# Dynamic convolution and two MLPs on one core: block 1's taps summed by TensorE, VectorE alone on the second weights, PSUM banks added one at a time, six blocks ahead, a new table of early tasks

## The chip, the cores and the metric

One core of a Trainium2 chip. The metric is device time in microseconds (us); lower is better. A profiled execution has its own time, and its trace covers a span a little shorter than that. Engines: PE (TensorE; PEld is its weight load), DVE (VectorE), ACT (ScalarE), POOL (GpSimd), and SP, which issues the DMAs. Each takes its instructions in the order in which the program lists them.

## The reference, cut to what matters

```python
# x (2, 4096, 192), weight_gen (2, 4096, 8, 7): float32, S = 4096, D = 192, H = 8, K = 7
w = softmax(weight_gen, axis=-1)                     # over the 7 taps
x_pad = np.concatenate([zeros((B, 6, D)), x], axis=1)
out[b, s, h, :] = sum_k w[b, s, h, k] * x_pad[b, s + k, h, :]     # 24 channels to a head
x = out.reshape(8192, 192)
x = (np.maximum(x @ w_in, 0.0) ** 2) @ w_out         # first MLP, 192 -> 2048 -> 192
h = x @ w_in2
return (h / (1.0 + np.exp(-1.702 * h))) @ w_out2     # second MLP
```

The four weight matrices arrive as float64 words.

## The kernel before, in words

**Tiling.** Token t of the flat 8192 lies on partition t // 64. The 64 tokens of a partition are cut into 16 blocks j of 4 (`TB`), so a block is 512 tokens. All matmul operands are split into a high part (rounded to `fp32r`) and a low part (the remainder); a product is the sum of three (high-high, low-high, high-low) or, in the second matrix, two of five column groups.

**A pair.** The unit of the main loop is (l, j, q): layer l, block j, one eighth q of the 2048 hidden columns. There are 2 x 16 x 8 = 256. For each, `mm_in` (L301) does 18 matmuls into a PSUM tile `h` of two banks; ACT makes `g` from it (L313 and L314: relu and square, or L316: gelu) and the high part `gh` (L320, `high_g`); DVE makes the low part `gl` (L326, `low_g`); and `mm_out` (L331) adds its product to the block's output `p`, two pairs later (`LAG`). For blocks 0 and 1 of layer 0 one `p` tile is used with 10 matmuls of 128 rows; everywhere else two `p` tiles, each from one half of the partitions, with 20 matmuls of 64 rows. `p0` and `p1` have one buffer each, two banks each, and a pool hands a tile on as a whole: the next block's first matmul into `p1` waits until both banks of the old `p1` have been read.

**Pair order.** L428 to L434: blocks 0 and 1 of layer 0 in two halves each (16 pairs), then layer 0 of the blocks below `LEAD`, then layer 1 of block j - `LEAD` alternating with layer 0 of block j, then the last `LEAD` blocks of layer 1. I number pairs from 0 in this order.

**Before a block's first pair.** `load_x` fetches the tokens and the six before them; `mul_task` multiplies by one tap's weights (L223, tile `pr`), `add` (L235) sums the seven products on DVE; `transposed` (L267) turns the sum with 16 small matmuls into a PSUM tile `tx` out of the same two buffers as `h`; `split` (L250) makes `xs`, high by ACT (L257), low by DVE (L258); `swap` (L261) copies halves across partitions by DMA. For block 0 alone (`plan_summed`, L461) the products are not added on DVE: each is transposed into the same PSUM tile, which adds them up. `softmax_tasks` (L173) make the tap weights `wg` for two blocks.

**Weights.** A `Chunk` (L88; 16 for each layer) is loaded, and then decoded from float64: ACT takes the magnitude (L104), DVE shifts and masks (L109, L110, L114: `t_bits`), multiplies and adds (L118, L121: `t_sum`), ACT rounds the high part (L138 or L156), DVE makes the low part (`wil`, L142; `wo`, L160 and L161). The addition of L121 runs on DVE for layer 0 and on POOL for layer 1.

**After a block's last pair.** `sums` (L349): ACT copies `p0` to `t` (L356) while DVE copies `p1` to `s` (L357); one step later DVE adds them (L363). Layer 0 then swaps and adds halves (L374, L378); layer 1 transposes (`u`, L407), and writes out (L412 to L420).

**Order of the work.** Every piece is a task in `todo`, keyed by a step; steps -20 to -1 come before the main loop, which has two steps to a pair: at the even step `low_g` of the pair before, `mm_in`, tasks; at the odd step `mm_out` of the pair two back, tasks, `high_g`. What an engine does, it does in that order. The numbers at L441 to L537 say at which step a task stands. `st` (L63) is one pool of ten buffers for raw weights, decoded weights, products, `s`, `t` and outputs.

Of the kernel before, what the change touches and what calls it, by code (L numbers as in the profile page):

```python
# [17 lines left out]
def kernel(  # L18
# [69 lines left out]
    class Chunk:  # L88
# [27 lines left out]
        def t_sum(self):  # L116
# [4 lines left out]
            (nc.vector if self.l == 0 else nc.gpsimd).tensor_add(self.s, self.s, self.u)  # L121
            del self.raw, self.low, self.high, self.u

        def tasks(self):
            return [self.t_words, self.t_bits, self.t_sum, self.t_high, self.t_low]
# [223 lines left out]
    def sums(l, j, hold):  # L349

        def t_copy():
            s = hold["s"] = work(f"s{l}_{j}", [P, 2, N])
# [1 line left out]
            if len(p) == 2:
                t = hold["t"] = work(f"t{l}_{j}", [P, 2, N])
                nc.scalar.copy(t, p[0])  # L356
                nc.vector.tensor_copy(s, p[1])  # L357
            else:
                nc.scalar.copy(s, p[j])

        def t_add():
            if "t" in hold:
                nc.vector.tensor_add(hold["s"], hold["s"], hold.pop("t"))  # L363

        return [t_copy, t_add]
# [95 lines left out]
    def plan_summed(j, i0, i1):  # L461

        hold = {}
        at(i0 - 6, lambda: hold.update(x=load_x(j)))
        for k in range(KT):
            at(
                i0 + k * (i1 - 2 - i0) // KT,
                mul_task(j, hold, k), lambda k=k: transposed(j, hold, k, k == 0, k == KT - 1),
            )
        at(i1 - 2, lambda: hold.pop("x"), *split_tasks(j, hold))  # L470

    def plan_softmax(s, i):
        at(i - 8, lambda: load_wg(s))
        for n, t in enumerate(softmax_tasks(s)):
            at(i + n, t)

    def plan_weights(chunk, when, lead):

        at(when[0] - lead, chunk.t_load)
        for t, i in zip(chunk.tasks(), when):  # L480
            at(i, t)
# [102 lines left out]
```

## Time and profile before

| | |
|---|---|
| median of 3 runs | 1212.54 us (1211.09 to 1214.18) |
| the profiled execution | 1212.81 us |
| its span in the trace | 1210.8 us |
| mean granted clock of TensorE | 0.981 |
| first matmul of pair 0 / of pair 16 / of pair 48 | 21.58 / 120.52 / 283.12 us |
| last matmul of pair 255 ends | about 1202.5 us |
| a pair where nothing waits | 4.31 us (blocks 0 and 1 of layer 0: 4.78 us) |

Three tables of the profile are read below. A row of the timeline is: start, duration, engine, source line, operation, output<-inputs, shapes, and in brackets how long the engine had been idle and what ended that. A row of the groups is a line's instructions of one kind: how many, busy us in total, mean ns of one, and the idle time of the engine before them. A row of the windows is one stretch of the span with each engine's busy time in it and the mean granted clock, 1.00 being 2.4 GHz and 0.50 being 1.2 GHz.

### The profile page before, as it was taken

How to read it: one execution, taken by the hardware profiler on the slowest of the kernel's cores; microseconds unless marked ns; L12 is line 12 of the kernel's file. 1: busy time of each engine (PE TensorE's matmuls, PEld its weight loads, DVE VectorE, ACT ScalarE, POOL GpSimd, SP SyncE). 2: the span in 40 equal slices, each digit the busy share in tenths (PEclk: the TensorE clock that was granted, in tenths of full speed). 3: DMA queues.
4: the chain of work that ended last, by engine and by line, in shares of the span. 5: the costliest groups of instructions: out<-in, count | busy, mean ns of one | idle time of the engine just before them, and what ended most of it. 6: DMA issues, size and time to landing. Idle time of an engine off the chain costs nothing.

```text
span 1210.8 us, 23439 instructions
## 1 busy us (share of the span) xinstructions
PE 1154.9 (95%) x10176; PEld 1087.1 (90%) x10176; DVE 723.0 (60%) x822; ACT 781.4 (65%) x821; POOL 30.8 (3%) x26
## 2 busy tenths in 40 slices
PE   4698899989999999999999999999999999999997
PEld 3466778879999999999999999998999999999997
DVE  7998897874646646465655646466464643433333
ACT  2676767857757675676757577576756757555553
POOL 1000111310000000000000000000000000000000
PEclk8899999989999999999999999999999999999999
DMA  7421223301121110112120011211101111110010
GB/s 189 113 88 41 88 63 120 87 9 52 31 60 39 41 41 19 52 41 58 32 59 27 23 51 32 60 39 41 41 19 51 34 24 32 28 31 15 18 32 27
DMA packets 29958, 58.90 MB, mean 49 GB/s; under 512 B 4004, under 2 KB 15394, under 8 KB 29856
## 3 DMA queue, kind: packets, MB, share of 16 engines
q1 hardware_dynamic: 29856, 57.41, 17.2%
q8 instruction: 79, 1.29, 0.5%
q14 instruction: 23, 0.19, 0.0%
HBM read 30.13 MB, written 6.29 MB: 30 GB/s over the span
## 4 chain that ended last, share of the span: by engine, by line
PE 83%; DVE 11%; ACT 2%; issue 2%; DMA 2%; SPq 0%; ACTq 0%; DVEq 0%
PE p L344 43%; PE h L307 38%; DVE pr L223 2%; DVE gl L326 2%; DVE pr L235 1%; DVE xs L258 1%; PE tx L278 1%; DMA xt<-in_x_dram 1%; PE u L407 1%; ACT xs L257 1%; ACT gh L320 1%; DMA ro<-in_moe_w_out_dram 1%; DVE uso L110 0%; DVE usi L110 0%; DVE usi L118 0%
## 5 line engine op out<-in xcount | busy, mean ns | idle before, releaser
L326 DVE TENSOR_TENSOR gl<-g,gh 128x1024 fp32r<-128x1024 f32 x256 | 317.3, 1239 | 327.2 <-ACT gh L320 326.9
L344 PE MATMUL p<-gh,wo 64*128 64x512 f32 (+1 forms) x2976 | 468.3, 392 | 11.0 <-DVE s L357 6.0
L307 PE MATMUL h<-xs,wih 64*128 64x512 f32 x3072 | 466.0, 392 | 7.3 <-DVE xs L258 4.1
L344 PEld LDWEIGHTS p<-gh,wo 64*128 64x128 f32 (+1 forms) x2976 | 344.9, 186 | 32.8 <-DVE s L357 7.1
L307 PEld LDWEIGHTS h<-xs,wih 64*128 64x128 f32 x3072 | 342.2, 186 | 30.3 <-PE p L344 7.8
L344 PE MATMUL p<-gl,wo 64*128 64x512 f32 (+1 forms) x1984 | 345.1, 389 | 0.0
L320 ACT CAST gh<-g 128x1024 fp32r<-128x1024 f32 x256 | 268.7, 1050 | 90.5 <-PE p L344 88.1
L344 PEld LDWEIGHTS p<-gl,wo 64*128 64x128 f32 (+1 forms) x1984 | 234.7, 186 | 10.2
L307 PE MATMUL h<-xs,wil 64*128 64x512 f32 x1536 | 231.0, 389 | 1.6 <-DVE wil L142 1.6
L316 ACT ACTIVATE g<-h 128x1024 f32<-128x1024 f32 x128 | 131.7, 1029 | 152.4 <-PE h L307 150.5
L313 ACT ACTIVATE g<-h 128x1024 f32<-128x1024 f32 x128 | 131.6, 1028 | 110.6 <-PE h L307 109.1
L307 PEld LDWEIGHTS h<-xs,wil 64*128 64x128 f32 x1536 | 173.0, 186 | 10.2 <-DVE wil L142 2.0
L314 ACT ACTIVATE g<-g 128x1024 f32<-128x1024 f32 x128 | 135.8, 1061 | 4.1
L223 DVE TENSOR_TENSOR pr<-xt,wg 128x768 f32<-128x768 f32 x112 | 107.0, 966 | 3.0 <-DMA xt<-in_x_dram 3.0
L235 DVE TENSOR_TENSOR pr<-pr,pr 128x768 f32<-128x768 f32 x90 | 87.1, 968 | 0.6
L357 DVE COPY s<-p 128x1024 f32<-128x1024 f32 x30 | 36.7, 1224 | 53.2 <-PE p L344 53.2
L356 ACT COPY t<-p 128x1024 f32<-128x1024 f32 x30 | 30.5, 1016 | 23.2 <-PE p L344 22.1
L278 PE MATMUL tx<-ident,pr 64*128 64x64 f32 x352 | 18.0, 254 | 28.5 <-DVE pr L223 14.1
L278 PEld LDWEIGHTS tx<-ident,pr 64*128 64x128 f32 x352 | 17.1, 164 | 31.3 <-DVE pr L223 14.6
L363 DVE TENSOR_TENSOR s<-s,t 128x1024 f32<-128x1024 f32 x30 | 36.6, 1219 | 0.1
L258 DVE TENSOR_TENSOR xs<-s,xs 128x1024 fp32r<-128x1024 f32 x16 | 19.6, 1226 | 25.4 <-ACT xs L257 25.4
L417 DVE TENSOR_TENSOR o<-u,ow 128x256 f32<-128x256 f32 x16 | 6.8, 425 | 31.3 <-ACT o L416 21.1
(46 smaller groups left out, 303.0 us busy)
## 6 DMA issues: line engine op xcount, KB each, us to landing
xs<-xs SPq DMA_DIRECT2D x128, 128.0 KB, 2.3
xt<-in_x_dram SPq DMA_DIRECT2D x14, 960.0 KB, 5.1
ri<-in_moe_w_in_dram SPq DMA_DIRECT2D x32, 192.0 KB, 3.5
ro<-in_moe_w_out_dram SPq DMA_DIRECT2D x16, 384.0 KB, 3.5
out_dram<-o SPq DMA_DIRECT2D x16, 384.0 KB, 2.3
w<-s SPq DMA_DIRECT2D x32, 128.0 KB, 2.3
wg<-in_weight_gen_dram SPq DMA_DIRECT2D x8, 224.0 KB, 2.8
xt<-in_x_dram SPq DMA_DIRECT2D x1, 768.0 KB
```

What stands on the lines that cost most here:

```text
L223: nc.vector.tensor_mul(pr, hold["x"][:, k:k + TB, :].rearrange("p t (h g) -> p t h g", h=H), wg_t[s][:, t0:t0 + TB, :, k:k + 1].to_broadca ...
L235: nc.vector.tensor_add(hold["p", 0], hold["p", 0], p)
L278: nc.tensor.matmul(out=hold["ps"][:, i, c:c + R], lhsT=cols, rhs=ident[rows, rows], is_transpose=True, start=(first and a == 0 and t == 0) ...
L307: nc.tensor.matmul(out=h[:, i, :], lhsT=w[HALVES[i], q, c, :], rhs=v[HALVES[i], n, PLACE[l][i][c], :], start=(o == 0), stop=(o == len(ops) ...
L313: nc.scalar.activation(out=g, in_=h, func=AF.Relu)
L314: nc.scalar.activation(out=g, in_=g, func=AF.Square)
L316: nc.scalar.activation(out=g, in_=h, func=AF.Gelu_apprx_sigmoid)
L320: nc.scalar.copy(gh, g_t[l, j, q])
L326: nc.vector.tensor_sub(gl, g, f32(gh))
L344: nc.tensor.matmul(out=p_t[l, j][i][:, a, :], lhsT=wo[l][rows, f, c:c + P], rhs=g[n][rows, e, :], start=(f == 0 and o in (0, 2)), stop=(f ...
L357: nc.vector.tensor_copy(s, p[1])
L363: nc.vector.tensor_add(hold["s"], hold["s"], hold.pop("t"))
```

## The change

What it does, in its five parts:

1. Block 1 is treated as block 0 was: seven products are transposed one after the other into one PSUM tile (`block_tasks`, `summed`), and the six additions on DVE are gone.
2. `t_sum` of the second layer's 16 chunks adds on DVE; POOL has no part in the weights any more.
3. `sum_task` takes the place of `sums`: ACT copies bank 0 of `p0`, DVE adds bank 0 of `p1` to it straight from PSUM, then the same for bank 1. The DVE copy of 1024 columns is gone, the addition is in two halves, and it stands at the step where the copies stood.
4. `LEAD` is 6 instead of 5: layer 1 begins eight pairs later (pair 48 instead of 40). Its chunks are planned every 4.5 steps instead of every 3.
5. A table `START` places the tasks of three softmaxes, three blocks and the first 16 chunks at fractions of a step. For later blocks transposition, high and low part stand together at an odd step, the block's first pair less 5 (they stood at less 6, 5 and 4). Buffers: `s`, `t` and the first layer's raw weights move to a pool `s` of seven; `st` has eight; `xin` and `sm` have one instead of two.

```diff
-    LEAD = 5
+    LEAD = 6
...
-    xin_p = ctx.enter_context(tc.tile_pool(name="xin", bufs=2))
+    xin_p = ctx.enter_context(tc.tile_pool(name="xin", bufs=1))
-    st_p = ctx.enter_context(tc.tile_pool(name="st", bufs=10))
-    sm_p = ctx.enter_context(tc.tile_pool(name="sm", bufs=2))
+    st_p = ctx.enter_context(tc.tile_pool(name="st", bufs=8))
+    s_p = ctx.enter_context(tc.tile_pool(name="s", bufs=LEAD + 1))
+    sm_p = ctx.enter_context(tc.tile_pool(name="sm", bufs=1))
...
-            raw = work(f"r{self.tag}", [P, 2 * CW], U32)
+            pool, tag = (s_p, "s") if self.l == 0 else (st_p, "st")
+            raw = pool.tile([P, 2 * CW], U32, tag=tag, name=f"r{self.tag}")
...
-            (nc.vector if self.l == 0 else nc.gpsimd).tensor_add(self.s, self.s, self.u)
+            nc.vector.tensor_add(self.s, self.s, self.u)
...
-        def t_copy():
-            s = hold["s"] = work(f"s{l}_{j}", [P, 2, N])
+        def f():
+            s = hold["s"] = s_p.tile([P, 2, N], F32, tag="s", name=f"s{l}_{j}")
             p = p_t.pop((l, j))
-            if len(p) == 2:
-                t = hold["t"] = work(f"t{l}_{j}", [P, 2, N])
-                nc.scalar.copy(t, p[0])
-                nc.vector.tensor_copy(s, p[1])
-            else:
+            if len(p) == 1:
                 nc.scalar.copy(s, p[j])
-
-        def t_add():
-            if "t" in hold:
-                nc.vector.tensor_add(hold["s"], hold["s"], hold.pop("t"))
-
-        return [t_copy, t_add]
+                return
+            t = s_p.tile([P, 2, N], F32, tag="s", name=f"t{l}_{j}")
+            for a in range(2):
+                nc.scalar.copy(t[:, a, :], p[0][:, a, :])
+                nc.vector.tensor_add(s[:, a, :], p[1][:, a, :], t[:, a, :])
+
+        return f
...
-        at(i1 - 6, lambda: hold.pop("x"), lambda: transposed(j, hold, 0, True, True))
-        high, low = split_tasks(j, hold)
-        at(i1 - 5, high)
-        at(i1 - 4, low)
+        load, *conv, turn, high, low = block_tasks(j, False)
+        at(i0 - 3, load)
+        spread(conv, i0, i1 - 6)
+        at(i1 - 5, turn, high)
+        at(i1 - 4.5, low)
...
+    START = {
...
+        "x1": (-6.64, -3.57, -3.52, -3.18, -0.17, -0.01, 0.4, 1.53, -3.56, -3.02, -2, 0.41, 0.96, 1.46, 2.3, 5.13, 5.14),
...
+        "i0": (-16.79, -16.78, -5.54, -5.53, -2.81, -1.74),
...
+    START_TASKS |= {f"x{j}": block_tasks(j, j < 2) for j in range(3)}
...
     for n in range(2 * NQ):
-        kind = (IN, OUT)[n % 2]
-        i = 4 * NQ + 4 + n * 3
-        plan_weights(kind(f"{kind.__name__[0].lower()}", 1, n // 2), (i, i + 1, i + 2, i + 4, i + 5), 4)
+        kind = (InChunk, OutChunk)[n % 2]
+        i = 4 * NQ + 4 + n * 4.5
+        plan(kind(kind.__name__[0].lower(), 1, n // 2).tasks(), (i - 4, i, i + 1, i + 2, i + 4, i + 5))
```

**PE at the program's start, before.** `tx0` and `tx1` are the transposed blocks 0 and 1, `pr1_k` tap k of block 1, `h0_0_1` the hidden tile of layer 0, block 0, q = 1; the numbers behind are the build's.

```order
7 L278 MATMUL tx0_118<-ident_82,pr0_6_250 128x64 x16
8 L307 MATMUL h0_0_0_309<-xs0_0_276,wih0_83 128x512 x6
9 L307 MATMUL h0_0_0_309<-xs0_0_276,wil0_85 128x512 x6
10 L307 MATMUL h0_0_0_309<-xs0_0_276,wih0_83 128x512 x6
11 L307 MATMUL h0_0_1_357<-xs0_0_276,wih0_83 128x512 x6
13 L307 MATMUL h0_0_1_357<-xs0_0_276,wih0_83 128x512 x6
14 L278 MATMUL tx1_379<-ident_82,pr1_0_290 128x64 x16
15 L307 MATMUL h0_0_2_417<-xs0_0_276,wih0_83 128x512 x6
```

The same place in the change:

```order
7 L281 MATMUL tx0_128<-ident_85,pr0_6_222 128x64 x16
8 L281 MATMUL tx1_297<-ident_85,pr1_0_295 128x64 x16
9 L281 MATMUL tx1_297<-ident_85,pr1_1_314 128x64 x16
10 L281 MATMUL tx1_297<-ident_85,pr1_2_316 128x64 x16
11 L310 MATMUL h0_0_0_377<-xs0_0_291,wih0_86 128x512 x6
12 L310 MATMUL h0_0_0_377<-xs0_0_291,wil0_88 128x512 x6
14 L281 MATMUL tx1_297<-ident_85,pr1_3_373 128x64 x16
16 L281 MATMUL tx1_297<-ident_85,pr1_5_399 128x64 x16
17 L310 MATMUL h0_0_1_464<-xs0_0_291,wih0_86 128x512 x6
20 L281 MATMUL tx1_297<-ident_85,pr1_6_453 128x64 x16
21 L310 MATMUL h0_0_2_524<-xs0_0_291,wih0_86 128x512 x6
```

Three taps of block 1 now stand ahead of pair 0, three ahead of pair 1 and one ahead of pair 2, where the finished sum stood ahead of pair 2.

**DVE at the end of a block, before** (layer 0, block 6: `p1_0_6` and `t0_6`):

```order
412 L326 TENSOR_TENSOR gl1_2_0_4238<-g1_2_0_4209,gh1_2_0_4236 128x1024
413 L235 TENSOR_TENSOR pr7_0_4005<-pr7_0_4005,pr7_4_4234 128x768
414 L357 COPY s0_6_4282<-p1_0_6_3894 128x1024
415 L326 TENSOR_TENSOR gl1_2_1_4288<-g1_2_1_4259,gh1_2_1_4286 128x1024
416 L223 TENSOR_TENSOR pr7_5_4311<-xt7_3841,wg3_2566 128x768
417 L363 TENSOR_TENSOR s0_6_4282<-s0_6_4282,t0_6_4283 128x1024
```

and in the change:

```order
405 L329 TENSOR_TENSOR gl1_1_0_3939<-g1_1_0_3910,gh1_1_0_3937 128x1024
406 L238 TENSOR_TENSOR pr7_0_3712<-pr7_0_3712,pr7_4_3935 128x768
407 L363 TENSOR_TENSOR s0_6_3983<-p1_0_6_3594,t0_6_3984 128x512 x2
408 L329 TENSOR_TENSOR gl1_1_1_3991<-g1_1_1_3960,gh1_1_1_3989 128x1024
409 L226 TENSOR_TENSOR pr7_5_4014<-xt7_3615,wg3_2173 128x768
```

Where one copy read `p1`, two additions of half its columns read it, and each takes its other operand from an ACT copy; the later addition is gone.

**DVE at the transposition of a block whose softmax falls beside it, before** (block 7, softmax 4):

```order
427 L189 TENSOR_REDUCE mx4_4434<-wg4_4232 128x64
429 L191 RECIPROCAL mx4_4434<-mx4_4434 128x64
430 L326 TENSOR_TENSOR gl1_2_5_4509<-g1_2_5_4460,gh1_2_5_4507 128x1024
431 L194 TENSOR_TENSOR wg4_4232<-wg4_4232,mx4_4434 128x448
432 L258 TENSOR_TENSOR xs0_7_4503<-tx7_4463,xs0_7_4503 128x2x8x64
433 L326 TENSOR_TENSOR gl1_2_6_4558<-g1_2_6_4530,gh1_2_6_4556 128x1024
```

and in the change:

```order
419 L192 TENSOR_REDUCE mx4_4136<-wg4_3933 128x64
421 L194 RECIPROCAL mx4_4136<-mx4_4136 128x64
422 L261 TENSOR_TENSOR xs0_7_4205<-tx7_4188,xs0_7_4205 128x2x8x64
423 L329 TENSOR_TENSOR gl1_1_5_4214<-g1_1_5_4162,gh1_1_5_4212 128x1024
424 L197 TENSOR_TENSOR wg4_3933<-wg4_3933,mx4_4136 128x448
425 L329 TENSOR_TENSOR gl1_1_6_4260<-g1_1_6_4235,gh1_1_6_4258 128x1024
```

The low part of `xs`, whose end frees the buffer of `tx`, now stands ahead of one `gl` and of a softmax product that it stood behind.

## Rows read from the trace of the kernel before

**Rows 1.** The page, part 1: busy time, share of the span, instructions.
```profile
PE 1154.9 (95%) x10176; PEld 1087.1 (90%) x10176; DVE 723.0 (60%) x822; ACT 781.4 (65%) x821; POOL 30.8 (3%) x26
```
**Rows 2.** Windows: stretch, length, busy of PE, PEld, DVE, ACT, POOL; clock, DMA share, GB/s.
```profile
21.58:120.52 98.94, 80.84 (x461) 57.24 (x462) 89.25 (x149) 64.50 (x81) 0.00 (x0) 0.89 0.31 85
120.52:283.12 162.60, 150.46 (x1246) 130.80 (x1246) 133.40 (x183) 116.07 (x134) 27.24 (x16) 0.95 0.27 77
283.12:1202.50 919.38, 916.49 (x8346) 892.80 (x8343) 484.18 (x466) 594.31 (x599) 0.00 (x0) 1.00 0.13 36
...
35.60:45.80 10.20, 5.98 (x36) 4.74 (x37) 9.92 (x20) 6.42 (x8) 0.00 (x0) 0.50 0.23 65
```
**Rows 3.** Waits of PE over the span: us in total, times, longest.
```profile
PE tx L278 <- DVE pr L235: 11.3, 3, 9.0
PE p L344 <- DVE s L357: 6.0, 3, 3.1
PE p L344 <- DVE wo L160: 5.0, 4, 3.3
PE h L307 <- DVE xs L258: 4.1, 6, 0.7
```
**Rows 4.** Groups of DVE and PE by line and form.
```profile
L223 DVE TENSOR_TENSOR pr<-xt,wg 128x768 f32<-128x768 f32 x112 | 107.0, 966 | 3.0 <-DMA xt<-in_x_dram 3.0
...
L278 PE MATMUL tx<-ident,pr 64*128 64x64 f32 x352 | 18.0, 254 | 28.5 <-DVE pr L223 14.1
```
**Rows 5.** Timeline of PE, first 60 us.
```profile
39.82 1.12 PE L278 MATMUL tx<-ident,pr 64*128 64x64 f32 x16 [8.99 <-DVE pr L235]
...
47.76 0.96 PE L307 MATMUL h<-xs,wih 64*128 64x512 f32 x6
```
**Rows 6.** The chain that ended last: start, us, what.
```profile
2.09 8.14 DMA xt<-in_x_dram
```
**Rows 7.** Timeline around block 7's low part: DVE, then PE.
```profile
415.92 0.55 DVE L191 RECIPROCAL mx<-mx 128x64 f32<-128x64 f32 x1
...
418.02 0.62 DVE L194 TENSOR_TENSOR wg<-wg,mx 128x448 f32<-128x448 f32 x1
418.56 1.22 DVE L258 TENSOR_TENSOR xs<-tx,xs 128x1024 fp32r<-128x1024 f32 x1
...
419.92 0.96 PE L307 MATMUL h<-xs,wih 64*128 64x512 f32 x6 [0.72 <-DVE xs L258]
```
**Rows 8.** Single lines and tiles: duration ns min/median/max, first and last start; who waited.
```profile
L326 DVE TENSOR_TENSOR gl<-g,gh x256: 1208/1226/2043, 41.1 to 1198.7; 128x1024 fp32r<-128x1024 f32 x128
...
L121 DVE TENSOR_TENSOR usi<-usi x8: 557/558/559, 16.5 to 85.2; 128x384 f32<-128x384 f32 x8
...
L121 POOL TENSOR_TENSOR usi<-usi x8: 1014/1596/4155, 139.1 to 246.9; 128x384 f32<-128x384 f32 x8
...
L378 DVE TENSOR_TENSOR s<-s,w x16: 684/693/1505, 119.6 to 1039.3; 128x512 f32<-128x512 f32 x16
...
L416 ACT COPY o<-u x16: 591/593/604, 305.5 to 1206.3; 128x512 f32<-128x512 f32 x16
```
**Rows 9.** Timeline of PE, three of the stops between pairs 16 and 48.
```profile
148.44 1.12 PE L278 MATMUL tx<-ident,pr 64*128 64x64 f32 x16 [3.09 <-ACT usi L104]
...
175.36 1.53 PE L344 MATMUL p<-gh,wo 64*128 64x512 f32 x5 [2.20 <-DVE s L357]
...
192.09 0.81 PE L278 MATMUL tx<-ident,pr 64*128 64x64 f32 x16 [1.90 <-DVE pr L235]
```
**Rows 10.** Timeline at an ordinary end of a block: the reads of `p`, the next `p`.
```profile
538.27 1.02 ACT L356 COPY t<-p 128x1024 f32<-128x1024 f32 x1 [1.21 <-PE p L344]
538.31 1.23 DVE L357 COPY s<-p 128x1024 f32<-128x1024 f32 x1 [1.54 <-PE p L344]
...
540.12 0.86 PE L344 MATMUL p<-gh,wo 64*128 64x512 f32 x6
```
**Rows 11.** Timeline at the program's end.
```profile
1205.24 0.72 PE L407 MATMUL u<-ident,s 64*128 64x64 f32 x16 [2.74 <-DVE s L363]
```

More of the change, by code (lines that the diff above doesn't have):

```diff
@@ L120, in t_sum @@
             )
[L121 removed]
+            nc.vector.tensor_add(self.s, self.s, self.u)
             del self.raw, self.low, self.high, self.u
         def tasks(self):
[L125 removed]
+            return [self.t_load, self.t_words, self.t_bits, self.t_sum, self.t_high, self.t_low]
     class InChunk(Chunk):
@@ L347, in mm_out, with sum_task @@
                     )
[L349 to L352 removed]
+    def sum_task(l, j, hold):
+        def f():
+            s = hold["s"] = s_p.tile([P, 2, N], F32, tag="s", name=f"s{l}_{j}")
             p = p_t.pop((l, j))
[L354 to L365 removed]
+            if len(p) == 1:
+                nc.scalar.copy(s, p[j])
+                return
[4 more added lines that the diff above has]
+        return f
     def first_tasks(j):
@@ L378, in t_sum @@
             nc.vector.tensor_add(s[:, 1, :], s[:, 1, :], hold.pop("w"))
-        return [*sums(0, j, hold), t_swap, t_sum]
+        return [sum_task(0, j, hold), t_swap, t_sum]
     def second_tasks(j):
@@ L420, in t_out @@
             )
-        return [*sums(1, j, hold), t_turn, t_out]
+        return [sum_task(1, j, hold), t_turn, t_out]
     turn = NQ // 2
@@ L444, in at @@
     def at(i, *tasks):
-        todo.setdefault(max(-PRE, i), []).extend(tasks)
+        i = max(-PRE, i)
+        todo.setdefault(int(i // 1), []).extend((i, t) for t in tasks)
     def spread(tasks, a, b):
@@ L449, in spread, with plan, block_tasks, softmax @@
             at(a + n * (b - a) // len(tasks), t)
-    def plan_block(j, i0, i1):
-        hold = {}
-        at(i0 - 6, lambda: hold.update(x=load_x(j)))
-        spread(conv_tasks(j, hold), i0, i1 - 6)
-        at(i1 - 6, lambda: hold.pop("x"), lambda: transposed(j, hold, 0, True, True))
-        high, low = split_tasks(j, hold)
-        at(i1 - 5, high)
-        at(i1 - 4, low)
[L461 to L481, printed above, removed]
+    def plan(tasks, when):
+        assert len(tasks) == len(when)
+        for t, i in zip(tasks, when):
+            at(i, t)
+    def block_tasks(j, summed):
+        hold = {}
+        load = lambda: hold.update(x=load_x(j))
+        if summed:
+            muls = [mul_task(j, hold, k) for k in range(KT)]
+            adds = [lambda k=k: transposed(j, hold, k, k == 0, k == KT - 1) for k in range(KT)]
+            muls[-1] = lambda f=muls[-1]: (f(), hold.pop("x"))
+            return [load, *muls, *adds, *split_tasks(j, hold)]
+        turn = lambda: transposed(j, hold, 0, True, True)
+        conv = conv_tasks(j, hold)
+        conv[-1] = lambda f=conv[-1]: (f(), hold.pop("x"))
+        return [load, *conv, turn, *split_tasks(j, hold)]
+    def plan_block(j, i0, i1):
+        load, *conv, turn, high, low = block_tasks(j, False)
[3 more added lines that the diff above has]
+        at(i1 - 4.5, low)
+    def softmax(s):
+        return [lambda: load_wg(s), *softmax_tasks(s)]
     def t_const():
@@ L548 @@
                 mm_out(*pairs[n - LAG])
-            for t in todo.pop(i, []):
+            for _, t in sorted(todo.pop(i, []), key=lambda it: it[0]):
                 t()
```

41 lines of the change are left out of this document (12 added, 29 removed), and 20 rows, old and new, of the table START.

## The prediction

> **What bounds the kernel now.** I read the page's busy shares first [rows 1]: PE is busy for 1154.9 of 1210.8 us, DVE 60%, ACT 65%. A share of 95% is an average, so I cut the span into stages at the first matmuls of pairs 0, 16 and 48 [rows 2]. From 283.12 us on PE idles 919.38 - 916.49 = 2.9 us: nothing but fewer matmuls can help there, and the change removes none. Before, it looks otherwise. Pairs 0 to 15 take 98.94 us; at 4.78 us a pair and 0.65 us for each of two transpositions 16 pairs need about 78. Pairs 16 to 47 take 162.60; 32 pairs of 4.31, three transpositions of 0.5 and 0.45 for two wide `mm_out` need 139.9, so 22.7 us are lost. The first 21.58 us are loads, one softmax and the taps of block 0. So some 43 us can be won, all before 283 us, and DVE is the engine that is busy there: 89.25 of 98.94 and 133.40 of 162.60. The waits of PE name it too [rows 3].
>
> The sum is made against the profiled execution, 1212.81 us, 2.0 above its span; the median of the runs is 1212.54, the same thing. About 0.3% (3.6 us) is what a measurement of this kernel can tell from no change.
>
> **Part A, block 1's taps and the order of the first 16 pairs.** PE gets 96 more small transposing matmuls, some 5 us (352 of them take 18.0 [rows 4]) in a stretch where it waits for DVE in any case; DVE loses six additions of 0.97 us. The order decides what comes of it. In the old order PE stood still for 8.99 us before the single transposition of block 1 [rows 5], and the 10.2 us that follow were granted 0.50, that is 1.2 GHz [rows 2]. In the new order that stop becomes three smaller ones, and the first is early. The tokens of block 0 land at 2.09 + 8.14 = 10.2 us [rows 6]. Seven products follow, each 0.97 us long [rows 4], one every 0.87, since DVE starts an instruction some 0.1 before the last one's end (418.56 against 418.02 + 0.62 [rows 7]): to 16.3. Then DVE has 14 decoding instructions of about the 0.56 us of L121 [rows 8] or less, 6 to 8 us, and the three products of block 1 that PE waits for: 25 us. So pair 0 starts about 4 us later than now. Five more sums, the low part of `xs` and a chunk's bits bring its low weights at about 30; it ends at 32; the next three taps take DVE to 35; pairs 1 and 2 at the low clock (4.2 us of `mm_in` each) and the first `mm_out` (2.5) bring pair 3 at about 47, where it starts now (47.76 [rows 5]). Up to there I see no gain.
>
> The gain is behind it. From there to pair 11 DVE is the bound: it idles 98.94 - 89.25 = 9.7 us in the whole stretch [rows 2], and PE waits for its weights (`wo`, 5.0 us [rows 3]). I count the old order up to the `gl` of pair 11 and the new one: the same softmaxes, the same chunks, but 31 tap products and additions against 21 (six additions gone, four tasks of block 2 put off). Ten at 0.87 are 8.7 us. At pair 12 it is seven, 6.1 us, but by then DVE no longer sets the end. I take **-8**. Bounds: -3, if the 4 to 5 us at the start are never made up; -12, if the low clock of [rows 2] also goes.
>
> **Part B, pairs 16 to 63.** The lost 22.7 us sit in some nine places; three are in [rows 9]. PE waits for a transposition that waits for a sum on DVE (192.09), for one that waits for ACT (148.44: ACT stands at `usi`, whose buffer DVE has not freed), for `p1`, which DVE copies late (175.36). A mean clock of 0.95 says besides that a tenth of the stretch, 16 us, ran at 1.2 GHz [rows 2]. The change makes more room: layer 1 is needed eight pairs later. By my count of the order, with DVE at 0.92 of its summed durations, the work in each stretch from `gl` to `gl` exceeds 4.31 us in a dozen places, by at most 2.6, and DVE's delay grows at most to some 3 us of the 4.3 that `gl` can be late before PE waits (two pairs less its own way). What is left is the end of block 2, where a chunk's bits stand ahead of the additions (0.9 us), block 3 (0.4), and four ends at the price of part C (0.8); I add 3 for what such a count does not see. It shows under 4 us on the old order, where 23 were lost. **-18** (23 to 5). Bounds: -21 and -3.
>
> The second weights alone on DVE are 16 x 0.558 = 8.9 us more work for it [rows 8]. Against that, beside POOL's additions (1.6 us each) a two-input instruction of DVE grew: `gl` to 2.04 at most where 1.23 is usual, L378 to 1.51 from 0.69 [rows 8]. At most 16 x 0.82 = 13 us come back, at least nothing; I take 9, so DVE's load stays as it is and the chain of decoding gets 1 us shorter a chunk. The Trainium skill ("SBUF — State Buffer", Who interferes with whom) has the two engines share one pair of ports under an exclusive lock, the loser blocked for a whole instruction. By that 16 x 1.6 = 26 us of DVE would be freed and B be nearer its better end; the 0.8 us that the rows show decide.
>
> **Part C, the end of a block.** Now `p1` is read in one copy: it starts at 538.31, takes 1.23, and the next `p` starts at 540.12, 0.58 us after it ends [rows 10]. In the change the chain is a half copy by ACT (0.59 [rows 8]), a half addition and a second. No row shows an addition of 512 columns out of PSUM; the nearest is L378 out of SBUF, 0.69, and a whole one takes 1.22 from either memory (L258 [rows 7] has PSUM as its source), so I take 0.69 with 0.08 of overlap, and bound it by 0.6 and 1.22. Chain: 538.27 + 0.59 + 0.61 + 0.69, with two handovers of 0.03 and 0.06: 540.25. That is 0.13 after 540.12. A short stop costs PE a little over its length (0.72 made a pair 0.91 longer [rows 7]), so 0.2, for the 23 ends from pair 64 to 255: **+4.6**. Bounds 0 and +12.
>
> **Part D, the low part of `xs`.** Four times behind pair 64, every 141 us from 420 on, PE waits 0.72 us for `xs` [rows 3, 7]; the pair takes 0.91 longer. There L258 starts at 418.56, behind a `gl` and a product; in the new order it stands right behind the reciprocal that ended at 416.5 (415.92 + 0.55) and can end at 417.7, while the step at which the buffer is needed stays. **-3.6**; bounds 0 and -3.6. **Part E, the last block:** `u` waits 2.74 us for copy and addition [rows 11]; by the chain of part C it waits 2.0: **-0.7**.
>
> More pieces with one answer: the DMAs keep their number; SP's queue now holds block 1's tokens until the last product of block 0 (one `xin` buffer), at 16.3, and they land by 22, about when DVE comes to them. Fewer `st` buffers: the tasks that wait for one wait for work at least a pair back.
>
> Sum: -8 - 18 + 4.6 - 3.6 - 0.7 = -25.7; 1212.8 - 25.7 = **1187 us**.
>
> **The rivals.**
>
> *1. The start stays cold (chance 0.10).* Pair 0's matmuls come later and between waits for taps. In the old trace PE ran at 1.2 GHz for 10.2 us around and after its 9 us of standing [rows 2, 5]. Twelve more such us would cost 6, and A would shrink to -2: 1193. The Trainium skill ("TensorE: Matmul & The Clock Gate", What's actually happening) says that the slow clock is the default and activity lifts it, which fits a start cut up by waits. Against it: from pair 1 on PE has work in a row.
>
> *2. DVE runs late between pairs 16 and 63 after all (0.14).* DVE would be busy for about 87% there, hardly less than in the old trace, and a late addition holds `p1`, a late tap sum holds PE. For it: my count explains too few of the old stops. Against: ACT no longer waits for buffers that DVE is just about to free, and POOL's detour is gone. With 20 of 23 us still lost: 1202.
>
> *3. The half additions are dear (0.05), the rival on the other side.* Each of 29 block ends makes PE wait for ACT, DVE, DVE in a row. If a half addition out of PSUM cost what a whole one does, 1.22, the chain would take 3.1 us in a window of 1.85, and each end 1.5 with the restart: 43.5 us in place of the 6.7 that parts B and C hold: 1224. It decides from 1.1 us an end. Against it: L378 takes 0.69 for this size.
>
> *4. Nothing in it (0.06).* The work put off from the first pairs comes back in the next stage, stop for stop: 1212.
>
> **How the numbers follow.** The forecast has 0.65: 1175 to 1196 by the bounds of A, B and C. Faster by over 0.3% is the forecast with rivals 1 and 2, 0.89, less a little for their ends: 0.87. Same 0.06, slower 0.07, where mishaps of the new buffers come in. The range takes in rivals 1 and 2: 1173 to 1205.
>
> **What would show it.** Pair 16 starts at about 112 us (120.52 now [rows 2]); at pair 64 PE is some 26 us ahead of the old trace, and from there to the end it keeps that lead, within 4. POOL shows no L121. L363 is 60 instructions of about 0.69. PE waits for L363 by 0.1 to 0.2 us at the block ends, and not for `xs` at 0.72. The prediction is wrong if pair 16 starts after 118 us (A), if PE loses over 12 us between pairs 16 and 64 (B), or if a block end costs over 0.5 us (C).

## The result and the profile after the change

The changed kernel takes 1180.65 us (median of 4 runs, 1179.05 to 1182.88), against 1212.6 us for the kernel before on the same chip: ratio 0.9738, 95% interval 0.9717 to 0.9758. The profiled execution took 1180.11 us with a span of 1178.0. That is 6 us faster than forecast and inside the range.

The page, part 1, of the changed kernel answers to [rows 1]; POOL has lost its 16 additions, and DVE, which took them over, is busy for 37 us less:

```profile
PE 1146.9 (97%) x10272; PEld 1056.3 (90%) x10272; DVE 686.1 (58%) x832; ACT 779.7 (66%) x849; POOL 3.7 (0%) x10
```

The windows of the changed kernel, cut at the same pairs as [rows 2] (columns as there):

```profile
28.47:109.67 81.20, 78.09 (x508) 55.82 (x509) 76.08 (x129) 61.65 (x76) 0.00 (x0) 0.96 0.35 98
109.67:253.36 143.69, 141.92 (x1246) 120.80 (x1246) 126.93 (x185) 117.36 (x134) 0.00 (x0) 1.00 0.30 85
253.36:1177.98 924.62, 918.30 (x8363) 871.66 (x8359) 461.79 (x485) 593.59 (x629) 0.00 (x0) 1.00 0.13 36
```

Pairs 0 to 15 take 81.20 us where they took 98.94, but the first begins 6.9 us later; pairs 16 to 47 take 143.69 for 162.60 and run at full clock, where 0.95 was granted. The last window ends at the span here, so its length doesn't compare with that of before.

What PE still waits for, over the span (total, times, longest), against [rows 3]:

```profile
PE tx L281 <- DVE pr L226: 17.6, 3, 10.5
PE p L347 <- DVE wo L163: 2.4, 3, 1.8
PE h L310 <- DVE xs L261: 2.2, 1, 2.2
PE p L347 <- DVE s L363: 1.7, 2, 1.1
PE u L407 <- DVE s L363: 1.6, 2, 1.2
```

The first row is the loading and the taps of the first two blocks, the last the program's end (2.74 in one stop before, [rows 11]). The sums of taps (11.3 us in three stops) and the low part of `xs` later on (six of up to 0.7) are gone. Between pairs 16 and 64 the kernel before had these waits (110 to 300 us):

```profile
PE p L344 <- DVE s L357: 6.0, 3, 3.1
PE tx L278 <- ACT usi L104: 3.1, 1, 3.1
PE tx L278 <- DVE pr L235: 1.9, 1, 1.9
PE h L307 <- DVE xs L258: 1.2, 2, 0.7
```

These are 12.2 us; the change has 1.7 there, in two stops for `s`.

To see where time is won, I take the start of the first matmul of `h` of a pair in PE's timeline of each trace, and subtract that of the changed kernel (so "before 10.85" under pair 16: the old kernel starts it 10.85 us later). Each row is one execution. What matters is the step from one column to the next:

| trace | pair 0 | 4 | 12 | 16 | 32 | 64 | 128 | 248 | end |
|---|---|---|---|---|---|---|---|---|---|
| before | -6.88 | 6.35 | 10.32 | 10.85 | 22.87 | 29.63 | 31.08 | 31.95 | 32.78 |
| u_pool | -0.58 | -0.58 | 0.99 | 0.77 | 0.80 | 0.81 | 0.89 | 0.83 | 0.83 |
| u_copy | 1.35 | 1.35 | 2.90 | 2.66 | 2.62 | 3.42 | 2.80 | 1.62 | 2.94 |
| u_lead | -0.78 | -0.74 | -0.76 | -0.70 | 4.39 | 9.14 | 9.15 | 9.07 | 9.09 |
| u_taps | -9.15 | 6.87 | 8.35 | 8.14 | 8.15 | 8.20 | 8.21 | 8.18 | 8.17 |
| u_three | -0.53 | -0.53 | -0.50 | -0.45 | 5.62 | 9.92 | 9.30 | 8.12 | 9.04 |
| u_lead_st11 | 2.72 | 2.75 | 4.28 | 4.04 | 9.98 | 14.69 | 14.66 | 14.51 | 14.53 |
| a_warm | 0.10 | -0.04 | 1.59 | 1.37 | 1.41 | 1.43 | 1.47 | 1.41 | 1.38 |
| a_early | -2.45 | -0.31 | 1.26 | 1.07 | 1.11 | 1.07 | 1.13 | 1.00 | 0.98 |
| u_step | -0.61 | -0.59 | -0.59 | -0.56 | 1.07 | 4.81 | 7.19 | 9.52 | 9.51 |
| u_three_step | -0.64 | -0.63 | -0.59 | -0.59 | 9.72 | 15.21 | 16.68 | 17.56 | 18.72 |
| best | -0.82 | -0.79 | 0.78 | 0.55 | -0.61 | -0.57 | -1.19 | -2.37 | -2.43 |
| best2 | 0.70 | 0.71 | -1.31 | 0.31 | -0.83 | -0.85 | -1.47 | -2.65 | -2.72 |

By the first row the change wins 10.85 us up to pair 16, 18.78 between pairs 16 and 64, 2.32 from there to pair 248, and 0.8 at the end. Of the 18.78, 10.5 are stops of PE that are gone (12.2 less 1.7). Some 8 more, an estimate, are the clock: 0.95 of it was granted over 162.60 us [rows 2], and 1.00 in the change.

One step of this table is chance. Ahead of pair 11 the changed kernel and all its variants but best2 stop for 1.80 to 1.88 us for the low part of `wo`. Behind that stop the granted clock is 0.50 for 3.4 us in seven of these twelve traces (u_pool, u_copy, u_taps, u_lead_st11, a_warm, a_early, best), and each of them loses 1.5 to 1.6 us between the columns of pairs 4 and 12. In the other five, the change's among them, it stays at 1.00 and nothing is lost there.

### The profile page after: what moved, and what is told of

It reads as the page before. It is cut to its first block, busy times and chain, and to the rows that moved or that the text cites. A ratio compares the mean times of both kernels' runs of the same rounds, so it can differ in the third digit from the quotient of the medians.

```text
span 1178.0 us, 23578 instructions
## 1 busy us (share of the span) xinstructions
PE 1146.9 (97%) x10272; PEld 1056.3 (90%) x10272; DVE 686.1 (58%) x832; ACT 779.7 (66%) x849; POOL 3.7 (0%) x10
## 3 DMA queue, kind: packets, MB, share of 16 engines
q8 instruction: 80, 1.31, 0.5%
## 5 line engine op out<-in xcount | busy, mean ns | idle before, releaser
L347 PE MATMUL p<-gh,wo 64*128 64x512 f32 (+1 forms) x2976 | 525.3, 388 | 4.1 <-DVE wo L163 2.4
L310 PE MATMUL h<-xs,wih 64*128 64x512 f32 x3072 | 524.1, 390 | 2.9 <-DVE xs L261 2.2
L347 PEld LDWEIGHTS p<-gh,wo 64*128 64x128 f32 (+1 forms) x2976 | 390.0, 184 | 37.9 <-DVE s L363 7.1
L310 PEld LDWEIGHTS h<-xs,wih 64*128 64x128 f32 x3072 | 391.5, 185 | 27.9 <-issue 2.5
L347 PE MATMUL p<-gl,wo 64*128 64x512 f32 (+1 forms) x1984 | 405.3, 387 | 0.0
L347 PEld LDWEIGHTS p<-gl,wo 64*128 64x128 f32 (+1 forms) x1984 | 285.4, 184 | 16.6
L310 PE MATMUL h<-xs,wil 64*128 64x512 f32 x1536 | 260.0, 388 | 0.0
L310 PEld LDWEIGHTS h<-xs,wil 64*128 64x128 f32 x1536 | 197.8, 185 | 11.3 <-DVE wil L145 0.7
L317 ACT ACTIVATE g<-g 128x1024 f32<-128x1024 f32 x128 | 135.9, 1062 | 4.1
L238 DVE TENSOR_TENSOR pr<-pr,pr 128x768 f32<-128x768 f32 x84 | 80.1, 954 | 1.1
L363 DVE TENSOR_TENSOR s<-p,t 128x512 f32<-128x512 f32 x60 | 38.6, 685 | 64.2 <-ACT t L362 64.2
L362 ACT COPY t<-p 128x512 f32<-128x512 f32 x60 | 32.3, 590 | 19.9 <-PE p L347 19.7
L281 PE MATMUL tx<-ident,pr 64*128 64x64 f32 x448 | 23.5, 254 | 17.8 <-DVE pr L226 17.6
```

Source lines behind the costliest of these rows:

```text
L238: nc.vector.tensor_add(hold["p", 0], hold["p", 0], p)
L281: nc.tensor.matmul(out=hold["ps"][:, i, c:c + R], lhsT=cols, rhs=ident[rows, rows], is_transpose=True, start=(first and a == 0 and t == 0) ...
L310: nc.tensor.matmul(out=h[:, i, :], lhsT=w[HALVES[i], q, c, :], rhs=v[HALVES[i], n, PLACE[l][i][c], :], start=(o == 0), stop=(o == len(ops) ...
L317: nc.scalar.activation(out=g, in_=g, func=AF.Square)
L347: nc.tensor.matmul(out=p_t[l, j][i][:, a, :], lhsT=wo[l][rows, f, c:c + P], rhs=g[n][rows, e, :], start=(f == 0 and o in (0, 2)), stop=(f ...
L363: nc.vector.tensor_add(s[:, a, :], p[1][:, a, :], t[:, a, :])
```

## The experiments

Times are medians; ratios are to the kernel before on the same chip, to be read against the change's 0.9738. Where an edit leaves the first tasks alone, a shift that is there from pair 0 on is the landing of the loads, which differs between executions.

### One part undone: POOL's additions (u_pool)

```diff
-            nc.vector.tensor_add(self.s, self.s, self.u)
+            (nc.vector if self.l == 0 else nc.gpsimd).tensor_add(self.s, self.s, self.u)
```

> The changed kernel (1180.7) with one part undone: the 16 additions of the second weights go back to POOL. Theory S (slack: what pairs 16 to 63 gained comes from the weights of layer 1 being due eight pairs later, and the engine of this addition does not matter): DVE sheds 16 x 0.56 = 8.9 us and gets about as much back by growing beside POOL, so 1178 to 1184, and pairs 16 to 63 last what they do now within 2 us. Rival P (POOL's detour and its lock were what stopped PE there): PE stands again in that stretch, 1187 or more. Rival Q (DVE is short of time there and POOL would relieve it): under 1178.

Measured: 1180.23 us, ratio 0.9747 (0.9727 to 0.9767). Between pairs 16 and 64 nothing happens (0.77 to 0.81). The windows over those pairs, first of this kernel, then of the change, say why:

```profile
110.44:324.38 213.94, 212.03 (x1885) 190.61 (x1886) 172.68 (x227) 167.41 (x190) 23.57 (x16) 1.00 0.26 73
```

```profile
109.67:323.56 213.89, 212.12 (x1885) 184.33 (x1886) 172.83 (x243) 167.48 (x190) 0.00 (x0) 1.00 0.26 73
```

DVE has 16 instructions fewer (227, 243) and the same busy time (172.68, 172.83): the 8.9 us that POOL takes over come back as growth of the instructions beside it. Theory S holds; P and Q fall. How the two engines hinder each other is seen in POOL's timeline and in DVE's:

```profile
148.12 1.61 POOL L124 TENSOR_TENSOR usi<-usi 128x384 f32<-128x384 f32 x1 [6.92 <-DVE usi L121]
```

```profile
147.90 0.95 DVE L238 TENSOR_TENSOR pr<-pr,pr 128x768 f32<-128x768 f32 x1
148.77 2.04 DVE L329 TENSOR_TENSOR gl<-g,gh 128x1024 fp32r<-128x1024 f32 x1
```

POOL's addition starts during L238 and ends 0.88 us after it; the next instruction of DVE takes 2.04 us where 1.22 is usual. Eleven of the 16 additions run so (1.56 to 1.88 us), the other five take 1.01 to 1.03; twelve instructions of DVE, all beside POOL, are 0.45 to 0.82 us longer than others of their kind. The Trainium skill ("SBUF — State Buffer", Who interferes with whom) has the engine that starts first hold a shared pair of ports for its whole instruction while the other one waits. The trace agrees, and by it POOL's 23.57 us hold POOL's own waits for DVE; DVE lost 8.8 us.

### One part undone: the old end of a block (u_copy)

```diff
-            t = s_p.tile([P, 2, N], F32, tag="s", name=f"t{l}_{j}")
-            for a in range(2):
-                nc.scalar.copy(t[:, a, :], p[0][:, a, :])
-                nc.vector.tensor_add(s[:, a, :], p[1][:, a, :], t[:, a, :])
+                t = hold["t"] = s_p.tile([P, 2, N], F32, tag="s", name=f"t{l}_{j}")
+                nc.scalar.copy(t, p[0])
+                nc.vector.tensor_copy(s, p[1])
...
+        def t_add():
+            if "t" in hold:
+                nc.vector.tensor_add(hold["s"], hold["s"], hold.pop("t"))
```

> The changed kernel (1180.7) with one part undone: at a block's end DVE copies p1 in one piece of 1.22 us and adds it to ACT's copy in a later task of 1.22. Theory S: a block end stops PE by 0.1 us more at 23 ends behind pair 64 (+2), and DVE has 1.2 us more work at each end, which five ends before pair 64 show by 0 to 3 us: 1181 to 1187. Rival E (the old copy, standing behind other work on DVE, was what stopped PE between pairs 16 and 63): 8 us or more come back before pair 64, 1189 or more.

Measured: 1180.12 us, ratio 0.9753 (0.9731 to 0.9775). It loses 0.8 between pairs 16 and 64, so rival E falls. Behind pair 64 I had the sign wrong: this kernel does not lose 2 us, it gains 1.8 (3.42 to 1.62 over 23 block ends, 0.08 each), and gives 1.3 back at the end of the program. The old copy is the cheaper end where DVE is free. The price of the new one is small, and the change's own timeline at such an end (compare [rows 10]) shows why:

```profile
507.96 1.07 ACT L362 COPY t<-p 128x512 f32<-128x512 f32 x2
...
508.58 1.29 DVE L363 TENSOR_TENSOR s<-p,t 128x512 f32<-128x512 f32 x2 [2.54 <-ACT t L362]
...
509.81 1.08 PE L347 MATMUL p<-gh,wo 64*128 64x512 f32 x6
509.92 0.52 PEld L347 LDWEIGHTS p<-gh,wo 64*128 64x128 f32 x5 [0.16 <-DVE s L363]
```

The second addition ends at 509.87 and PE's next `p` is hardly held: not a matmul but a weight load waits, 0.16 us, while the matmul ahead of it still runs. Behind pair 64 this is all that there is (waits of PEld, 300 to 1170 us, changed kernel; u_copy has none):

```profile
PEld p L347 <- DVE s L363: 3.8, 24, 0.2
```

### One part undone: five blocks ahead (u_lead)

```diff
-    LEAD = 6
+    LEAD = 5
...
-        i = 4 * NQ + 4 + n * 4.5
+        i = 4 * NQ + 4 + n * 3
```

The pool `s` keeps its seven buffers.

> The changed kernel (1180.7) with one part undone: layer 1 starts five blocks behind layer 0, no longer six, and a chunk of its weights is planned every 3 steps, no longer every 4.5. Theory S: pairs 16 to 63 lose 10 to 18 of the 18.8 us that they gained, pairs 0 to 15 and those from 64 on stay within 1 us: 1190 to 1199. Rivals P and E (POOL's additions or the old sums were the cause, and the room of eight pairs is beside the point): 1185 or less.

Measured: 1190.21 us, ratio 0.9837 (0.9813 to 0.9861). Pairs 16 to 63 lose 9.84 us and nothing else moves, so theory S is right, a little under the lower edge that I gave that stretch: this part is half of what the change won there. The waits of PE between 110 and 300 us grew from 1.7 us in two stops (changed kernel) to

```profile
PE p L347 <- DVE s L363: 7.6, 3, 3.7
```

and the timeline of DVE at the longest shows the new half additions last in a queue of decoding and taps:

```profile
157.03 0.56 DVE L124 TENSOR_TENSOR usi<-usi 128x384 f32<-128x384 f32 x1
157.51 0.95 DVE L226 TENSOR_TENSOR pr<-xt,wg 128x768 f32<-128x768 f32 x1
158.50 0.96 DVE L238 TENSOR_TENSOR pr<-pr,pr 128x768 f32<-128x768 f32 x1
159.37 1.28 DVE L363 TENSOR_TENSOR s<-p,t 128x512 f32<-128x512 f32 x2
```

With two more of 0.2 us these waits are 6.3 us longer than in the change. The other 3.5 are the clock, which is 0.50 for 3.4 us behind each of two of the stops (162.1 to 165.5, 237.2 to 240.6) and 1.00 in the change.

### One part undone: block 1's taps (u_taps)

```diff
-    START_TASKS |= {f"x{j}": block_tasks(j, j < 2) for j in range(3)}
+    START_TASKS |= {f"x{j}": block_tasks(j, j < 1) for j in range(3)}
```

The 17 numbers of `x1` are put in the order product, product, addition, and so on; each addition keeps the place that its transposition had.

> The changed kernel (1180.7) with one part undone: the taps of block 1 are added on DVE at the places where PE now adds them, and transposed once; the rest of the new order stays. Theory D (DVE sets the time up to pair 11): six additions of 0.87 us come back there, pair 16 starts 4 to 6 us later, 1185 to 1188. Rival O (the order alone gained it, DVE has room): pair 16 within 1.5 us of now, 1182 or less. Rival C (the clock): PE stands again for several us before pair 4, is granted 1.2 GHz behind it, and pair 16 comes 8 us or more later, 1188 or more.

Measured: 1188.47 us, ratio 0.9817 (0.9798 to 0.9837). Pair 0 starts 9.2 us earlier; pair 4 is 6.9 us later, pair 10 6.7, pair 16 8.1. Up to the start of pair 10 DVE is busy for 74.59 us, where it is 69.30 in the change: 5.3 of the 6.7 are the six additions, as theory D has it. The other 1.4 are idle time of DVE. It idles 2.4 us in one stretch behind a stop of PE of 6.84 us for the sum of the taps (windows of u_taps, the second with the clock at 0.65 and DVE busy for 4.58 of 6.94 us):

```profile
33.22:44.09 10.87, 4.03 (x36) 3.07 (x34) 10.73 (x17) 7.80 (x10) 0.00 (x0) 0.66 0.28 63
44.09:51.03 6.94, 6.94 (x34) 5.08 (x30) 4.58 (x9) 2.65 (x4) 0.00 (x0) 0.65 0.00 0
```

The step from 6.7 to 8.1 comes at the stop for `wo` (1.88 us here, 1.83 in the change), behind which the clock is 0.50 from 89.9 to 93.3 us. By the table that is chance and not the taps. So theory D has 5.3 us and theory C at most 1.4; rival O falls. The kernel before, whose clock also fell there (97.0 to 100.4 us), shows what the new order is worth without the taps: nothing up to pair 10 (6.48 against 6.71), and 10.85 - 8.14 = 2.7 us at pair 16.

### Three parts undone together (u_three)

The edits of u_pool, u_copy and u_lead in one kernel.

> Three parts undone together (POOL adds the second weights, the old copy and addition at a block's end, layer 1 five blocks behind and a chunk every 3 steps); the order of the first tasks, the taps of block 1 on PE and the separate buffers stay. Undone one by one they lost 0.1, 0.8 and 9.8 us between pairs 16 and 64, of the 18.8 that the change gained there. Theory I (each stands in for the other: DVE has room enough with any one of them): together they lose 15 us or more there, 1196 or more. Rival N (they only add up, and the other 8 us come from the buffers and the order of block 2): 10 to 12 us, 1190 to 1194.

Measured: 1191.22 us, ratio 0.9834 (0.9806 to 0.9862). Between pairs 16 and 64 it loses 10.4 us. The parts add up (0.0 + 0.8 + 9.8); rival N, and 8 of the 18.8 us are still without a cause.

### Fewer buffers (u_lead_st11)

```diff
-    st_p = ctx.enter_context(tc.tile_pool(name="st", bufs=8))
-    s_p = ctx.enter_context(tc.tile_pool(name="s", bufs=LEAD + 2))
+    st_p = ctx.enter_context(tc.tile_pool(name="st", bufs=11))
```

This is u_lead with one more change: `s`, `t` and the first layer's raw words draw on the one pool too.

> The kernel with layer 1 five blocks behind (1190.2, of which pairs 16 to 63 hold 9.8 us more than the change), and its two sets of working buffers, 8 and 7, made one of 11 (10 before the change, which this order does not allow). Theory B (the other 8 us of pairs 16 to 63 came from buffers: in the kernel before, ACT stood 3.1 us at a buffer of a chunk at 148 us): ACT stands at buffers again and PE with it, 4 to 8 us more, 1194 to 1199. Rival N (buffers don't matter there): within 1.5 us of 1190.2.

Measured: 1194.3 us, ratio 0.9864 (0.9832 to 0.9896). The time looks like theory B, and the trace says otherwise: of the 5.4 us that it is behind u_lead at the end, 3.5 are lost before pair 4 and 1.2 up to pair 16; pairs 16 to 63 take 10.65 us more than in the change, only 0.8 more than u_lead. PE's waits of 110 to 300 us are the same as in u_lead:

```profile
PE p L346 <- DVE s L362: 7.6, 3, 3.7
```

The 0.8 are the clock (10.2 us at 0.50 there, 6.8 in u_lead), and the 1.2 are the clock behind the stop for `wo`. Theory B falls for the stretch that it was about. Before pair 0 buffers do count: the first products start 1.0 us later (10.15, 9.14), and two products of block 1 then wait 1.2 us each for PE's transposition of the product before; what that frees is the product's buffer. Eleven buffers are one more than the kernel before had; ten were not run.

### The steps of blocks 3 to 15 (u_step)

```diff
-        at(i1 - 5, turn, high)
-        at(i1 - 4.5, low)
+        at(i1 - 6, turn)
+        at(i1 - 5, high)
+        at(i1 - 4, low)
```

> The changed kernel (1180.7) with the steps of blocks 3 to 15 undone: transposition at i1 - 6, high part at i1 - 5, low part at i1 - 4, as before the change. By the run with the old copies a block end costs 0.09 us more in the change, 2.0 in all behind pair 64; the change gained 2.3 there, so theory D puts 4.3 us on this step: behind pair 64 the time grows by 3.5 to 4.5, with PE waiting 0.72 us for xs every 141 us; ahead of it 0 to 3 us more. 1184 to 1188. Rival: the step is worth nothing and the ends cost nothing, 1182 or less.

Measured: 1191.21 us, ratio 0.9834 (0.9814 to 0.9854). Behind pair 64 it loses 4.7 us, all of it at the four blocks where the waits of 0.7 are back, 1.17 to 1.21 us each (waits of PE, 300 to 1187 us):

```profile
PE h L310 <- DVE xs L261: 2.9, 4, 0.7
```

Ahead of pair 64 it loses 5.4, more than expected. 3.9 of that lie between pairs 36 and 40. Timelines of PE and of DVE in this kernel:

```profile
210.20 0.71 PE L281 MATMUL tx<-ident,pr 64*128 64x64 f32 x16 [2.19 <-ACT g L317]
```

```profile
208.82 0.36 DVE L117 TENSOR_SCALAR usi<-usi 128x384 uint32<-128x384 uint32 x1
209.10 0.95 DVE L238 TENSOR_TENSOR pr<-pr,pr 128x768 f32<-128x768 f32 x1
```

The last addition of the taps stands on DVE behind a softmax and a chunk's bits and ends at 210.05; the transposition starts 0.15 us later. The releaser that the row names, ACT's L317, is not what the transposition reads. From 211.1 to 214.5 us the granted clock is 0.50. So the stop of 2.19 us and the clock behind it make up the 3.9.

### The same on top of the three parts (u_three_step)

> The kernel with three parts undone (1191.2) and the steps of blocks 3 to 15 undone as well. Of the 18.8 us that the change gained between pairs 16 and 64, 10.4 are lost in the former. In the kernel before the change two stops there (148.44 and 192.09 us) were transpositions that waited for the last addition of a block's taps. Theory T (the transposition half a pair later is what lets that addition finish): 6 to 8 us come back between pairs 16 and 32, and 4 behind pair 64: 1199 to 1204. Rival R (the order of block 2 and the softmaxes did it): only the 4 behind pair 64, 1194 to 1196.

Measured: 1198.27 us, ratio 0.9894 (0.987 to 0.9919). Between pairs 16 and 64 it loses 15.8 us, 5.4 more than u_three: 4.2 of them up to pair 32, where theory T wanted 6 to 8 and rival R nothing. Its waits of PE bring the old stops back:

```profile
PE tx L281 <- DVE pr L238: 3.6, 2, 1.9
```

With this, the two stops of the kernel before can be read anew. Its timelines of DVE and POOL at 148.44 and 192.09 us [rows 9]:

```profile
147.34 0.95 DVE L235 TENSOR_TENSOR pr<-pr,pr 128x768 f32<-128x768 f32 x1
```

```profile
189.54 1.59 POOL L121 TENSOR_TENSOR usi<-usi 128x384 f32<-128x384 f32 x1 [7.16 <-ACT uso L104]
190.31 1.63 DVE L235 TENSOR_TENSOR pr<-pr,pr 128x768 f32<-128x768 f32 x1
```

Both times the sum of a block's taps ends (148.29; 191.94, grown beside POOL) 0.15 us before PE's transposition starts. ACT's L104, which the first row of [rows 9] names, had begun at 147.88 us without idling before it. Half a pair more for that sum is what the new steps give.

### The clock at the start (a_warm)

```diff
+    at(-7.04, t_warm(140))
+    at(-1.99, t_warm(40))
```

`t_warm(m)` issues m transpositions of the 64 x 64 identity into the bank of `p1`, which is not yet in use.

> The changed kernel (1180.7) with 140 and 40 extra small transpositions of the identity, 0.04 us each, in the two waits of PE before pair 0 (16.5 to 23.4 us, 26.2 to 28.5 us); their result is not used. There the granted clock fell to 0.50, from 18.1 to 35.2 us. Theory D (DVE sets the time up to pair 11): with the clock at 1.00 pairs 1 and 2 start 2 to 3 us earlier, DVE makes PE wait for it afterwards, pair 16 starts within 1 us of now and the time is 1179.5 to 1182. Rival C (the low clock at the start is what is left to win): the 2 to 3 us are kept to the end, 1177 to 1178.5.

Measured: 1181.88 us, ratio 0.9756 (0.9728 to 0.9785). The granted clock is now 1.00 through the whole start; pairs 1 to 3 begin 0.9 to 1.1 us earlier, and from pair 4 to pair 10 the two traces agree within 0.05 us. Rival C falls: DVE has the time there. Then, ahead of pair 11, both kernels stop for the low part of `wo`. PE in the changed kernel, then in this one:

```profile
82.79 0.74 PE L347 MATMUL p<-gh,wo 128*128 128x512 f32 x2 [1.83 <-DVE wo L163]
...
83.82 0.84 PE L347 MATMUL p<-gh,wo 128*128 128x512 f32 x3
```

```profile
82.79 0.73 PE L347 MATMUL p<-gh,wo 128*128 128x512 f32 x2 [1.87 <-DVE wo L163]
...
83.89 1.48 PE L347 MATMUL p<-gh,wo 128*128 128x512 f32 x3
```

The same stop, 1.83 and 1.87 us, ending at the same time; the second is followed by 3.4 us at 0.50 (83.7 to 87.1), and that puts pair 12 1.6 us later. Three kernels whose program is the change's own up to there (u_pool, u_copy, best) show the same fall, so the warm start is not needed for it; what decides it these traces do not show.

### Pair 0 earlier (a_early)

```diff
-        "x0": (..., -7.05, -3.77, -2.26),
+        "x0": (..., -7.05, -3.77, -3.06),
```

> The changed kernel (1180.7) with one task earlier: the low part of block 0 on DVE ahead of four decoding instructions, not behind them. Pair 0 waits for its buffer until that instruction ends (28.3 us); it can now start at 26.3. Theory D (DVE sets the time up to pair 11, and its work is the same): pair 0 is 2 us earlier, pair 16 within 1 us of now, 1179.5 to 1182. Rival F (the first pair's start carries through): all pairs 2 us earlier, 1178.5 or less.

Measured: 1180.96 us, ratio 0.9752 (0.9726 to 0.9778). Pair 0 starts 2.45 us earlier, because its PSUM buffer, which the low part of block 0 reads, is free earlier; PE then waits for the low weights instead:

```profile
26.01 0.98 PE L310 MATMUL h<-xs,wih 64*128 64x512 f32 x6
29.77 1.65 PE L310 MATMUL h<-xs,wil 64*128 64x512 f32 x6 [2.78 <-DVE wil L145]
```

By pair 4 0.3 us are left; ahead of pair 12 the clock falls behind the stop for `wo`, as in a_warm, and this kernel is 1.3 us later there. Theory D again.

### A better version (best, best2)

```diff
+        if last[l, j] < 2 * 56 or (l, j) == (1, NB - 1):
+            return [sum_task(l, j, hold)]
...
+        return [t_copy, t_add]
...
-        i = 4 * NQ + 4 + n * 4.5
+        i = 4 * NQ + 4 + n * 4.5 + (n == 3)
```

`t_copy` and `t_add` are the old end of a block. best2 changes besides three numbers of `x2`, from 16.13, 16.14 and 18.59 to 19.95, 20.5 and 21.5.

> The changed kernel (1180.7) with the old copy and addition for the block ends from pair 56 on, the last one left as changed, and the second layer's chunk 3 one step later, so that its bits stand behind the additions at the end of block 2 (PE stops 1.10 us there). By the runs so far: 2.0 us less behind pair 64, 1 to 1.4 less at the end of block 2: 1177 to 1178.7. Rival: the chunk meets other work of DVE at its new place and gives the 1.4 back, 1178.7 to 1180.

> The kernel of the run before it, with three tap instructions of block 2 on DVE put behind the low part of the fifth chunk of wo (PE waits 1.8 us for it ahead of pair 11). Theory D (DVE sets the time up to pair 11): 2.6 us of work less ahead of that wait, 1 to 2 us gained at pair 16: 1175.5 to 1177.5. Rival: block 2 is then late for pair 16, and nothing is gained, 1177 to 1179.

Measured: 1177.9 us, ratio 0.9722 (0.97 to 0.9744), and 1176.58 us, ratio 0.9715 (0.9697 to 0.9733). The intervals overlap with that of the change (0.9717 to 0.9758); what makes the gain credible is its places. The loss of the stop at the end of block 2 is down by 1.2 us (0.55 to -0.61 between pairs 16 and 32), and the ends behind pair 64 bring 1.8. best2 wins 2.0 us up to pair 12 and gives 1.6 back at once, where PE stops for 1.5 us for the next chunk of `wo`; at pair 16 0.4 are left of the 1 to 2 that theory D wanted. Against best, on which it is built, it is 1.7 us, but 1.6 of them are the clock, which fell behind the stop for `wo` in the trace of best and not in this one. Block 2 is not late, so its rival falls too: the stop only moved on.

## Why the prediction was right, and where it was off

**Part A, -8 forecast, -10.9 measured.** The mechanism held: nothing that happens on PE before pair 4 matters (a_warm, a_early), and six additions fewer on DVE are 5.3 us of the gain (u_taps). Up to pair 10 6.5 us are won, where the count of DVE's instructions gave 8.7 up to the `gl` of pair 11. The other 4.4 come between pairs 10 and 16. There the old kernel stood for 0.69, 3.27 and 0.41 us, twice for `wo` [rows 3] and once for a sum of taps, and the change once for 1.83: 2.5 us. And the old kernel was granted 0.50 for 3.4 us (97.0 to 100.4 us), the change 1.00: 1.6 us by a_warm. That term was not in the sum, and it is luck, since the clock fell at this place in seven of twelve traces of the changed kernel and its variants. Had it fallen in the change's trace too, the change would be some 9.3 us ahead. The bound of -12 named another stretch at the low clock, that of [rows 2], which runs from 35.6 to 45.8 us and so begins within the stop of 8.99 us, not behind it.

**The course of the start was wrong in detail.** Pair 0 came at 28.5, not 25 to 26: I counted what the matmuls read and missed that their PSUM buffer is the one that block 0's low part has still to read (a_early moves it, and pair 0 follows). Pair 3 came at 43.7, not 47: I had pairs 1 and 2 at 1.2 GHz, and the clock was back at 34.9 us. Rival 1, the cold start, did come about (17.1 us at 0.50, from 17.8 to 34.9), and cost nothing: with the clock at 1.00 there, DVE set the same time for pair 4 (a_warm).

**Part B, -18 forecast, -18.8 measured: the right sum for partly the wrong reason.** The room of eight pairs is 9.8 of it (u_lead). 5.4 are the new steps of the transposition and the low part (u_step), which the prediction had only in part D, for the low part and the time behind pair 64. The step that failed is the reading of the stop at 148.44 us: "ACT stands at `usi`, whose buffer DVE has not freed", taken from the releaser's name. It was the sum of taps on DVE, and with four buffers fewer PE's waits stayed the same there (u_lead_st11). The old block end is 0.8 and POOL 0.0; with all four undone together 15.8 of the 18.8 us go (u_three_step). Of the last 3.0 no part was tried alone, and their cause stays open: the order of block 2 and of the softmaxes and the number of buffers are in it.

**POOL's additions, nothing forecast, nothing measured,** by the account given: DVE's load stayed as it was, to 0.15 us. The prediction took 9 us to come back to DVE, and 8.8 did; the 26 us that it set beside this counted POOL's own waiting as DVE's loss.

**Part C, +4.6 forecast, +1.8 measured.** The half addition was sized rightly; the groups of the changed kernel:

```profile
L363 DVE TENSOR_TENSOR s<-p,t 128x512 f32<-128x512 f32 x60 | 38.6, 685 | 64.2 <-ACT t L362 64.2
```

The chain ended where it was put, 1.91 us after ACT's start against 1.98. What failed is the price of a stop: 0.2 us for 0.13 of waiting, taken from a matmul that waits. Here a weight load waits, 0.16 us, beside a running matmul, and a block end costs 0.08 us more than the old one. Rival 3 was never near.

**Part D, -3.6 forecast, -4.1 to -4.7 measured** (2.32 + 1.8 from the table, or u_step). That is beyond its bound of -3.6: a stop costs 1.17 to 1.21 us and not 0.91, since in u_step the pair itself is 0.94 longer and each of the two beside it about 0.1. **Part E, -0.7 forecast, -0.8 measured.**

## What to carry to other kernels

Before costing an edit to an engine that waits, find which engine sets the time in that stretch and count its instructions up to the point where the others catch up: work taken off it there stays won, and an earlier start or a higher clock of an engine that waits for it does not. Where the work order is a table of steps, a step's place decides as much as its cost: moving a block's transposition half a pair back and its low part half a pair forward was worth 10 us here, 5.4 ahead of pair 64 and 4.7 behind it. A releaser's name is a hint; look which of the operands ended just before the start. Before two traces are compared, look whether the clock fell in one of them alone.
